# One read-out per chunk: the weights' products of all eight tiles in one PSUM bank

## The chip, the cores and the metric

The kernel runs on one core of a Trainium2 chip. The metric is the device time of one execution in microseconds; lower is better. Engines are named as in the profile: PE is the matrix engine (PEld its weight loads), DVE the vector engine, ACT the scalar engine, POOL the GpSimd engine, SP the engine whose queue issues most DMAs.

## The reference

Three stages follow one another, all in float32. Only the first is touched by the change:

```python
# r, k, v, w, a, b: [4, 8, 768, 40]  (batch, heads, time, dim)
for t in range(S):
    y[:, :, t] = np.einsum('bhd,bhde->bhe', rt, state)
    Sa = np.einsum('bhde,bhe->bhd', state, at)
    state_decay = state * wt[:, :, None, :] - np.einsum('bhd,bhe->bhde', Sa, bt)
    state = state_decay + np.einsum('bhd,bhe->bhde', vt, kt)
```

The second stage is a gated feed-forward block: `h = relu(x @ w_in)`, a convolution over three time steps, a sigmoid gate, `(h * gate) @ w_out`. The third is a causal attention with four experts of which each token uses two.

## The kernel before, in words

**Tiling.** The recurrence is computed in chunks of 32 time steps. `NT` = 12 blocks of 64 steps hold `NC` = 2 chunks each, so there are 24 chunks, k = 0 to 23. The 32 pairs of batch and head lie as 8 tiles (`NP`), each with two heads times two sides on the partitions.

**Streams.** The recurrence is written as generators, each of which yields the time at which its next piece is due (one block of 64 steps is 1.0): `prep(n)` makes the decay products and the triangular inverse of a block, mostly on DVE; `chain(k)` carries the state from chunk to chunk, mostly on PE and ACT; `post(k)` reads the outputs of a chunk out of the state; `ff` is the feed-forward stage, which starts while the recurrence still runs. `Kernel.merge` always takes the stream with the earliest due time and emits its next piece; `ff` is put in whenever the PE work counted so far (the first arguments of `mm` and `tr`) calls for it. So the order of the yields sets the order in which instructions are emitted; the framework's scheduler then orders them for each engine by its own estimate of when each is ready, and puts in the semaphores. On the chip each engine runs its instructions in that order. PSUM is one tensor of 8 banks of 512 float32 columns; `self.ps[j]` are pairs of banks.

**The read-out, `post(k)`**, due from k/2 + 0.5 on over half a block. It copies keys and state into `LB` by DMA, turns `U` with four transposes into `vp` and copies them to `VT` on ACT (L438). Then, for tiles 0 to 3 and again for tiles 4 to 7 (`p0` = 0 and 4):

- the weights' products (`ra` with `VT`, 8 matmul calls of 64x64) go into half a PSUM bank (256 columns), `ap`;
- two DVE multiplications (L448, one for each 64 partitions) bring them under the causal mask into `RB`.

After that the loads of `ra` and `VT` for the next chunk are issued, and again for `p0` = 0 and 4:

- the sums (`LB` with `RB`, 16 matmul calls) go into a half bank, `yp`;
- one DVE multiplication (L463) by the decay `P` writes them to `xe`.

Then the next `RB` is loaded, and after each second chunk `xe` goes to DRAM (L470), from where the feed-forward stage picks it up as `xd` (L537). Each matmul call in float32 appears as two MATMUL records. For chunks k >= 3 (`BK`) both products and sums of tiles 0 to 3 use the lower half of the bank `po` (the second bank of `ps[3]`), those of tiles 4 to 7 its upper half. For the first three chunks tiles 0 to 3 use `po` (products below, sums above) and tiles 4 to 7 a bank of `ps[1]`, which the feed-forward stage does not need yet. The memsets in `setup_a` clear the rows of these half banks that no sum writes and that the scaling reads.

Of the kernel before, what the change touches and what calls it, by code (L numbers as in the profile page):

```python
# [13 lines left out]
ALU = mybir.AluOpType  # L14
# [7 lines left out]
NP, NC = 8, 2  # L22

LEAST = float(np.array(0x38100000, np.int32).view(np.float32))
POST, FF, W0, W1, HB, WB, WT, REST, LW, LS, LT, LV, LR, LAG, BURST, Y0, Y1, EN, Y2, XA, GM, SC, UD, WF, WK, WS, WX, WD, WR, WV, WA, WY, GN, BK, FZ, FN, KQ, GU, LO = 0.5, 1.4, 0.2, 1, 4, 1, 12000, 1, 3.5, 1.0, 0.6, 0, -1.48, 1, 0.8, -0.4, 1.0, 3, 0, 30, 1, 0, 0, 20, 25, 34, 42, 59, 25, 54, -13, -29, 0, 3, 0, 3, 1, 0, 0
R = (slice(0, 40), slice(64, 104))
Z = (slice(0, 64), slice(64, 128))
E = slice(0, 104)
# [21 lines left out]
class Kernel:  # L50
# [7 lines left out]
    def setup_a(self, ctx):  # L58
        tc, nc = self.tc, self.nc
        cp = self.cp = ctx.enter_context(tc.tile_pool(name="acst", bufs=1))  # L60
        self.wk = ctx.enter_context(tc.tile_pool(name="awk", bufs=2))
        self.w = cp.tile([128, 32, 32], F32, name="w")
        self.kb = cp.tile([128, 16, 2, 2, 32], F32, name="kb")

        self.a = [cp.tile([128, 2, 2, 16, 32], F32, name=f"a{j}") for j in range(2)]
        self.SV = cp.tile([128, 2, 2, NP, 40], F32, name="SV")
        self.ra = cp.tile([128, NP, 2, 2, 32], F32, name="ra")

        self.LB = [cp.tile([128, 2, NP, 2, 40], F32, name=f"LB{j}") for j in range(2)]
        self.RB = cp.tile([128, 2, NP, 2, 32], F32, name="RB")  # L70
        self.P = [cp.tile([128, 32, 32], F32, name=f"P{j}") for j in range(3)]

        self.U = [cp.tile([128, NP // 2, 104], F32, name=f"U{j}") for j in range(2)]
        self.VZ = cp.tile([128, NP, 2, 2, 40], F32, name="VZ")
        self.VT = cp.tile([128, NP, 2, 64], F32, name="VT")
        self.sT = [cp.tile([128, NP, 104], F32, name=f"sT{j}") for j in range(2)]
        self.S = [cp.tile([128, NP, 2, 40], F32, name=f"S{j}") for j in range(2)]
        self.g21 = cp.tile([128, 8, 2, 16], F32, name="g21")
        self.d1 = cp.tile([128, 8, 32], F32, name="d1")
        self.M1 = cp.tile([128, 8, 2, 16], F32, name="M1")  # L80
        self.po = self.ps[3][:, 1].rearrange("p (a b) -> p a b", a=2)
        nc.vector.memset(self.w[32:64], 1.0)
        nc.gpsimd.memset(self.kb[32:64], 0.0)
        nc.gpsimd.memset(self.a[0][32:64], 0.0)
        nc.vector.memset(self.P[0][:, :, 0:1], 1.0)
        nc.vector.memset(self.po[:, 1], 0.0)
        nc.vector.memset(self.ps[1][:, 1, 256:], 0.0)
        cst = cp.tile([128, 164], F32, name="cst")
        self.ident, self.mask = cst[:, :128], cst[:, 128:160]
        self.m0, self.m1, self.m2 = cst[:, 160:161], cst[:, 161:162], cst[:, 162:163]  # L90
        self.cst = cst
        self.t = {}
        self.work = self.nn = 0
# [322 lines left out]
    def post(self, k):  # L416
        nc, wk, t = self.nc, self.wk, self.t[k // NC]
        n, c = divmod(k, NC)
        P, VT = t["P"], self.VT
        ra, LB, RB, u0 = self.ra, self.LB[k % 2], self.RB, NP * c  # L420
        for be in range(2):
            h = slice(64 * be, 64 * be + 64)
            nc.sync.dma_start(LB[h, be].rearrange("p u a d -> p (u a d)"), t["KB"][h, u0:u0 + NP].rearrange("p u a d -> p (u a d)"))
            if k:
                nc.sync.dma_start(LB[R[1 - be], be].rearrange("p u a d -> p (u a d)"),
                                  self.S[k % 2][R[be]].rearrange("p u a d -> p (u a d)"))
        if c == 0:
            t["xe"] = wk.tile([128, NP, 2, TOK], F32, name="xe", bufs=1)
        def po(p0, j):

            if k < BK:
                return (self.ps[1][:, 1].rearrange("p (a b) -> p a b", a=2) if p0 else self.po)[:, j]
            return self.po[:, p0 // 4]

        vp = (self.ps[1] if k < BK else self.ps[3])[:, 0].rearrange("p (u x) -> p u x", u=4)
        for p in range(4):
            self.tr(WV, vp[E, p], self.U[k % 2][:, p], self.ident)
        nc.scalar.activation(VT[E].rearrange("p u b x -> p (u b) x")[:, :, 32:], vp[E].rearrange("p u (b t) -> p (u b) t", t=32), AF.Copy)  # L438
        yield 0.16
        for p0 in range(0, NP, 4):  # L440
            ap = po(p0, 0).rearrange("p (u a t) -> p u a t", u=4, a=2)
            for p in range(4):
                for be in range(2):
                    self.mm(WA, ap[64 * be:64 * be + 64, p], VT[E, p0 + p, be], ra[E, p0 + p, be], start=True, stop=True)
            for be in range(2):
                s = slice(64 * be, 64 * be + 64)
                y = RB[s, be, p0:p0 + 4].rearrange("p u a t -> p (u a) t")
                nc.vector.tensor_tensor(y, ap[s].rearrange("p u a t -> p (u a) t"), self.mask[s, None].to_broadcast([64, 8, 32]), op=ALU.mult)  # L448
            yield 0.3 + 0.04 * p0
        if k + 1 < NT * NC:  # L450
            self.load_ra(k + 1)
            self.load_vt(k + 1)
        for p0 in range(0, NP, 4):
            yp = po(p0, 1).rearrange("p (m b t) -> p m b t", m=4, b=2)
            for p in range(4):
                for be in range(2):
                    r = slice(0, 104 + 24 * be)
                    for al in range(2):
                        self.mm(WY, yp[R[al], p, be], LB[r, be, p0 + p, al], RB[r, be, p0 + p, al], start=True, stop=True)
                if p % 2 == 1:  # L460
                    yield 0.55 + 0.05 * (p0 + p)
            pp = P.rearrange("p (c m b) t -> p c m b t", c=NC, b=2)[E, c, p0:p0 + 4]
            nc.vector.tensor_tensor(t["xe"][E, p0:p0 + 4, :, 32 * c:32 * c + 32], yp[E], pp, op=ALU.mult)  # L463
            yield 0.72 + 0.05 * p0
        if k + 1 < NT * NC:
            self.load_rb(k + 1)
        if c:
            xs = self.dp.tile([4, 2, 40, B, TOK], F32, name="xs", bufs=3)
            for al in range(2):
                nc.sync.dma_start(xs[:, al].rearrange("q e b t -> e b q t"),  # L470
                                    t["xe"][R[al]].rearrange("p (b h) c t -> p b (h c) t", b=B))
            t["xs"] = xs
        yield 1.0
# [557 lines left out]
```

## Time and profile before

| what | value |
|---|---|
| median of 3 runs | 901.09 us (898.76 to 907.43) |
| the profiled execution | 902.53 us, of which the span from the first to the last instruction is 900.8 us |
| busy: PE, PEld, DVE, ACT, POOL (whole span) | 756.9, 659.8, 699.4, 571.3, 365.6 us |
| mean granted PE clock | 0.929 of full speed |
| masking instructions L448 | 96, first at 73.3 us, last at 582.7 us |
| scaling instructions L463 | 48, first at 79.6 us, last at 586.2 us |

The read-out of the chunks runs from about 72 to 587 us; behind it the last pieces of the feed-forward stage and the attention follow, up to 900.8 us. The busy times are averages over stages with different limits: only what the first 587 us show bears on the change directly.

### The profile page before, as it was taken

How to read it: one execution, taken by the hardware profiler on the slowest of the kernel's cores; microseconds unless marked ns; L12 is line 12 of the kernel's file. 1: busy time of each engine (PE TensorE's matmuls, PEld its weight loads, DVE VectorE, ACT ScalarE, POOL GpSimd, SP SyncE). 2: the span in 40 equal slices, each digit the busy share in tenths (PEclk: the TensorE clock that was granted, in tenths of full speed). 3: DMA queues.
4: the chain of work that ended last, by engine and by line, in shares of the span. 5: the costliest groups of instructions: out<-in, count | busy, mean ns of one | idle time of the engine just before them, and what ended most of it. 6: DMA issues, size and time to landing. Idle time of an engine off the chain costs nothing.

```text
span 900.8 us, 31560 instructions
## 1 busy us (share of the span) xinstructions
PE 756.9 (84%) x13112; PEld 659.8 (73%) x13112; DVE 699.4 (78%) x1614; ACT 571.3 (63%) x1353; POOL 365.6 (41%) x419
## 2 busy tenths in 40 slices
PE   1257667988889988898988889959889989999988
PEld 1156556777778877787877779858778878888876
DVE  6888698798798989899898794656567776786664
ACT  1156556676676748584857577657767666776665
POOL 6163443434333324344333235564434353344353
PEclk9999568998898889998998899979999999999999
DMA  5434574545454556553646355250011100110001
GB/s 128 105 121 115 139 170 106 132 101 136 104 132 113 122 130 146 120 128 77 146 108 152 68 121 118 48 143 28 10 45 37 45 16 31 37 38 16 17 15 37
DMA packets 143488, 81.17 MB, mean 90 GB/s; under 512 B 113858, under 2 KB 127042, under 8 KB 142386
## 3 DMA queue, kind: packets, MB, share of 16 engines
q1 hardware_dynamic: 138450, 74.34, 33.8%
q0 software_dynamic: 4896, 4.83, 2.4%
q8 instruction: 103, 1.69, 0.8%
q14 instruction: 39, 0.32, 0.1%
HBM read 51.63 MB, written 11.80 MB: 70 GB/s over the span
## 4 chain that ended last, share of the span: by engine, by line
PE 38%; DVE 29%; ACT 10%; DMA 9%; issue 6%; POOL 4%; SPq 3%; POOLq 0%; ACTq 0%; DVEq 0%
PE ps L163 8%; PE ps L720 4%; DVE cv L604 4%; PE ps L823 4%; PE ps L569 4%; PE ps L806 4%; PE ps L592 3%; PE ps L167 2%; PE ps L770 2%; DVE RB L448 2%; PE ps L711 2%; DVE Q L200 2%; PE ps L838 2%; PE ps L771 2%; DVE a L211 2%
## 5 line engine op out<-in xcount | busy, mean ns | idle before, releaser
L792 POOL TENSOR_TENSOR A<-A,rs 128x128 f32<-128x128 f32 (+5 forms) x96 | 87.7, 936 | 106.3 <-DVE rs L790 61.3
L607 POOL TENSOR_TENSOR cv<-cv,h 128x512 f32<-128x512 f32 (+1 forms) x48 | 59.1, 1230 | 150.0 <-ACT cv L606 129.0
L604 DVE SCALAR_TENSOR_TENSOR cv<-h,cw,cv 128x256 f32<-128x256 f32 (+1 forms) x192 | 97.1, 546 | 25.0 <-ACT cv L602 21.9
L569 PE MATMUL ps<-xh,win 128*128 128x256 f32 x384 | 94.3, 302 | 5.8 <-ACT xh L545 4.2
L569 PE MATMUL ps<-xl,win 128*128 128x256 f32 x384 | 95.1, 300 | 0.5 <-POOL xl L546 0.4
L592 PE MATMUL ps<-wout,gh 128*128 128x320 f32 x384 | 90.5, 331 | 5.8 <-ACT gh L486 5.5
L777 ACT ACTIVATE A<-ps,nm 128x128 f32<-128x128 f32 (+5 forms) x96 | 60.8, 634 | 35.8 <-DVE nm L775 26.8
L487 POOL TENSOR_TENSOR gl<-cv,gh 128x512 fp32r<-128x512 f32 x48 | 62.6, 1305 | 44.6 <-ACT gh L486 44.0
L569 PEld LDWEIGHTS ps<-xh,win 128*128 128x128 f32 x384 | 71.3, 204 | 7.9 <-ACT xh L545 4.7
L592 PEld LDWEIGHTS ps<-wout,gh 128*128 128x128 f32 x384 | 66.2, 201 | 8.3 <-ACT gh L486 6.8
L569 PEld LDWEIGHTS ps<-xl,win 128*128 128x128 f32 x384 | 70.9, 202 | 1.8 <-POOL xl L546 0.8
L775 DVE TENSOR_REDUCE nm<-ps 128x1 f32<-128x128 f32 (+5 forms) x96 | 58.6, 619 | 16.9 <-PE ps L773 10.8
L163 PE MATMUL ps<-kb,a 40*32 40x64 f32 x1536 | 39.2, 254 | 32.7 <-DVE kb L207 29.4
L592 PE MATMUL ps<-wout,gl 128*128 128x320 f32 x192 | 59.4, 332 | 0.9 <-POOL gl L487 0.9
L163 PE MATMUL ps<-RB,LB 104*40 104x32 f32 (+1 forms) x1536 | 50.6, 213 | 11.1 <-DVE RB L448 6.9
L163 PEld LDWEIGHTS ps<-kb,a 40*32 40x32 f32 x1536 | 30.9, 129 | 37.6 <-issue 19.2
L163 PEld LDWEIGHTS ps<-RB,LB 104*40 104x40 f32 (+1 forms) x1536 | 42.2, 127 | 20.5 <-DVE RB L448 9.0
L720 PE MATMUL ps<-x,wqk 128*128 128x384 f32 x256 | 54.5, 353 | 2.8 <-DVE lg L714 2.4
L606 ACT ACTIVATE cv<-cv 128x512 f32<-128x512 f32 (+1 forms) x48 | 30.3, 630 | 39.8 <-DVE cv L604 39.5
L806 PE MATMUL ps<-cid,A 128*128 128x128 f32 x336 | 53.0, 277 | 2.2 <-POOL A L792 1.5
L770 PE MATMUL ps<-k,q 128*128 128x256 f32 (+3 forms) x144 | 49.5, 352 | 3.6 <-ACT A L777 3.3
L163 PE MATMUL ps<-ra,VT 104*64 104x64 f32 x768 | 43.8, 255 | 8.4 <-DVE RB L448 6.8
(178 smaller groups left out, 2177.7 us busy)
## 6 DMA issues: line engine op xcount, KB each, us to landing
kb<-in_kb_e_dram SPq DMA_DIRECT2D x24, 320.0 KB
LB<-KB SPq DMA_DIRECT2D x48, 160.0 KB
LB<-S SPq DMA_DIRECT2D x46, 100.0 KB
a<-in_a_e_dram SPq DMA_DIRECT2D x24, 160.0 KB
VT<-in_vt_dram SPq DMA_DIRECT2D x48, 80.0 KB
RB<-in_rb_dram SPq DMA_DIRECT2D x48, 80.0 KB
SV<-in_v_dram SPq DMA_DIRECT2D x48, 80.0 KB
VZ<-in_v_dram SPq DMA_DIRECT2D x96, 40.0 KB
```

The costliest lines, as they stand in the source:

```text
L163: self.nc.tensor.matmul(*a, **k)
L487: (eng or self.nc.vector).tensor_tensor(lo, x, hi.bitcast(F32), op=ALU.subtract)
L569: nc.tensor.matmul(hp[:, dd], wt[:, 128 * d:128 * d + 128], x, start=k == 0, stop=k == 7)
L592: nc.tensor.matmul(self.ps[1][:, tb, :DM], x, wt, start=d == 0 and k == 0, stop=d == 7 and k == 2)
L604: nc.vector.scalar_tensor_tensor(y, h[:, dd, :, k:k + nt], self.cw[:, k, d:d + 1], y, op0=ALU.mult, op1=ALU.add)
L607: (nc.gpsimd if GM and st % GM == 0 and st >= GN else nc.vector).tensor_tensor(cv[:, :, :, :nt], cv[:, :, :, :nt], h[:, :, :, 1:1 + nt], o ...
L720: nc.tensor.matmul(pp, self.wqk[:, wk, hl, 128 * m:128 * m + 128], x[:, xk], start=j == 0, stop=j == 7)
L770: nc.tensor.matmul(sp[:, c0:c1], q[:, ce, 128 * j:128 * j + 128], k[:, ce, c0:c1], start=True, stop=False)
L775: nc.vector.tensor_reduce(nm, sp[:, :nk], axis=AX.X, op=ALU.max, negate=True)
L777: nc.scalar.activation(A[:, :nk], sp[:, :nk], AF.Exp, bias=nm, accum_out=sums[:, e:e + 1])
L792: nc.gpsimd.tensor_tensor(A[:, :nk], A[:, :nk], rs[:, e:e + 1].to_broadcast([128, nk]), op=ALU.mult)
L806: nc.tensor.transpose(tp[:, m, e], As[e][:, 128 * (2 * g + m):128 * (2 * g + m) + 128], self.cid)
```

## The change

The two halves of the read-out become one. All eight tiles' products fill one whole bank (the second of `ps[3]`, 512 columns), two masking instructions of 64x512 follow, then all eight tiles' sums fill a whole bank (for the first three chunks one of `ps[1]`, later the same bank of `ps[3]`), and one scaling instruction of 104x512 follows. The matmuls, the DMAs and their counts stay as they were. The yields become fewer: within the products there is one after tile 3 (0.3), the masking is emitted behind the last product; the sums yield after tiles 3 and 7 (0.70 and 0.90), where they yielded after each second tile (0.60, 0.70, 0.80, 0.90). The two memsets of half a bank become one of a bank.

```diff
--- before.py
+++ after.py
@@ -78,13 +78,11 @@
         self.g21 = cp.tile([128, 8, 2, 16], F32, name="g21")
         self.d1 = cp.tile([128, 8, 32], F32, name="d1")
         self.M1 = cp.tile([128, 8, 2, 16], F32, name="M1")
-        self.po = self.ps[3][:, 1].rearrange("p (a b) -> p a b", a=2)
         nc.vector.memset(self.w[32:64], 1.0)
         nc.gpsimd.memset(self.kb[32:64], 0.0)
         nc.gpsimd.memset(self.a[0][32:64], 0.0)
         nc.vector.memset(self.P[0][:, :, 0:1], 1.0)
-        nc.vector.memset(self.po[:, 1], 0.0)
-        nc.vector.memset(self.ps[1][:, 1, 256:], 0.0)
+        nc.vector.memset(self.ps[1][:, 1], 0.0)
         cst = cp.tile([128, 164], F32, name="cst")
         self.ident, self.mask = cst[:, :128], cst[:, 128:160]
         self.m0, self.m1, self.m2 = cst[:, 160:161], cst[:, 161:162], cst[:, 162:163]
@@ -426,42 +424,36 @@
                                   self.S[k % 2][R[be]].rearrange("p u a d -> p (u a d)"))
         if c == 0:
             t["xe"] = wk.tile([128, NP, 2, TOK], F32, name="xe", bufs=1)
-        def po(p0, j):
-
-            if k < BK:
-                return (self.ps[1][:, 1].rearrange("p (a b) -> p a b", a=2) if p0 else self.po)[:, j]
-            return self.po[:, p0 // 4]
-
         vp = (self.ps[1] if k < BK else self.ps[3])[:, 0].rearrange("p (u x) -> p u x", u=4)
         for p in range(4):
             self.tr(WV, vp[E, p], self.U[k % 2][:, p], self.ident)
         nc.scalar.activation(VT[E].rearrange("p u b x -> p (u b) x")[:, :, 32:], vp[E].rearrange("p u (b t) -> p (u b) t", t=32), AF.Copy)
         yield 0.16
-        for p0 in range(0, NP, 4):
-            ap = po(p0, 0).rearrange("p (u a t) -> p u a t", u=4, a=2)
-            for p in range(4):
-                for be in range(2):
-                    self.mm(WA, ap[64 * be:64 * be + 64, p], VT[E, p0 + p, be], ra[E, p0 + p, be], start=True, stop=True)
+        ap = self.ps[3][:, 1].rearrange("p (u a t) -> p u a t", u=NP, a=2)
+        for p in range(NP):
             for be in range(2):
-                s = slice(64 * be, 64 * be + 64)
-                y = RB[s, be, p0:p0 + 4].rearrange("p u a t -> p (u a) t")
-                nc.vector.tensor_tensor(y, ap[s].rearrange("p u a t -> p (u a) t"), self.mask[s, None].to_broadcast([64, 8, 32]), op=ALU.mult)
-            yield 0.3 + 0.04 * p0
+                self.mm(WA, ap[64 * be:64 * be + 64, p], VT[E, p, be], ra[E, p, be], start=True, stop=True)
+            if p == 3:
+                yield 0.3
+        for be in range(2):
+            s = slice(64 * be, 64 * be + 64)
+            y = RB[s, be].rearrange("p u a t -> p (u a) t")
+            nc.vector.tensor_tensor(y, ap[s].rearrange("p u a t -> p (u a) t"), self.mask[s, None].to_broadcast([64, 2 * NP, 32]), op=ALU.mult)
+        yield 0.46
         if k + 1 < NT * NC:
             self.load_ra(k + 1)
             self.load_vt(k + 1)
-        for p0 in range(0, NP, 4):
-            yp = po(p0, 1).rearrange("p (m b t) -> p m b t", m=4, b=2)
-            for p in range(4):
-                for be in range(2):
-                    r = slice(0, 104 + 24 * be)
-                    for al in range(2):
-                        self.mm(WY, yp[R[al], p, be], LB[r, be, p0 + p, al], RB[r, be, p0 + p, al], start=True, stop=True)
-                if p % 2 == 1:
-                    yield 0.55 + 0.05 * (p0 + p)
-            pp = P.rearrange("p (c m b) t -> p c m b t", c=NC, b=2)[E, c, p0:p0 + 4]
-            nc.vector.tensor_tensor(t["xe"][E, p0:p0 + 4, :, 32 * c:32 * c + 32], yp[E], pp, op=ALU.mult)
-            yield 0.72 + 0.05 * p0
+        yp = (self.ps[1] if k < BK else self.ps[3])[:, 1].rearrange("p (m b t) -> p m b t", m=NP, b=2)
+        for p in range(NP):
+            for be in range(2):
+                r = slice(0, 104 + 24 * be)
+                for al in range(2):
+                    self.mm(WY, yp[R[al], p, be], LB[r, be, p, al], RB[r, be, p, al], start=True, stop=True)
+            if p % 4 == 3:
+                yield 0.55 + 0.05 * p
+        pp = P.rearrange("p (c m b) t -> p c m b t", c=NC, b=2)[E, c]
+        nc.vector.tensor_tensor(t["xe"][E, :, :, 32 * c:32 * c + 32], yp[E], pp, op=ALU.mult)
+        yield 0.92
         if k + 1 < NT * NC:
             self.load_rb(k + 1)
         if c:
```

## Rows read from the trace of the kernel before

**Rows 1.** Stretches: us, busy time (and instructions) per engine, granted clock, DMA

```profile
core 0: us, PE busy (x) PEld busy (x) DVE busy (x) ACT busy (x) POOL busy (x), PEclk, DMA share, GB/s
60.00:120.00 60.00, 42.65 (x880) 34.93 (x882) 48.52 (x108) 36.25 (x78) 24.65 (x30) 0.72 0.50 130
200.00:300.00 100.00, 90.27 (x2153) 79.29 (x2155) 86.66 (x185) 67.53 (x148) 35.28 (x39) 0.90 0.51 119
400.00:500.00 100.00, 85.12 (x2026) 75.94 (x2011) 91.43 (x185) 67.75 (x150) 38.15 (x41) 0.91 0.54 125
800.00:901.00 101.00, 93.67 (x817) 78.32 (x815) 62.43 (x183) 61.53 (x164) 42.36 (x46) 0.99 0.08 26
```

**Rows 2.** Chain that ended last: start, us, what; first and last of L448, L463

```profile
104.64 0.38 DVE RB L448
...
116.51 0.33 DVE xe L463
...
582.71 0.44 DVE RB L448
...
586.19 0.43 DVE xe L463
```

**Rows 3.** One chunk's read-out in time: start, us, engine, line, operation [idle before]

```profile
338.63 0.33 PE L163 MATMUL ps<-ra,VT 104*64 104x64 f32 x2
...
339.70 0.85 DVE L448 TENSOR_TENSOR RB<-ps,cst 64x256 f32<-64x256 f32 x2
...
341.67 0.69 PE L163 MATMUL ps<-ra,VT 104*64 104x64 f32 x16
...
343.95 0.86 DVE L448 TENSOR_TENSOR RB<-ps,cst 64x256 f32<-64x256 f32 x2
...
345.63 0.50 PE L163 MATMUL ps<-RB,LB 104*40 104x32 f32 x16
...
350.47 0.43 DVE L463 TENSOR_TENSOR xe<-ps,P 104x256 f32<-104x256 f32 x1
...
350.95 0.80 PE L163 MATMUL ps<-RB,LB 104*40 104x32 f32 x32 [1.21 <-DVE xe L463]
```

**Rows 4.** By line: ns min/median/max of masking, scaling, a 512-column multiplication

```profile
L448 DVE TENSOR_TENSOR RB<-ps,cst x96: 371/427/431, 73.3 to 582.7; 64x256 f32<-64x256 f32 x96
L463 DVE TENSOR_TENSOR xe<-ps,P x48: 376/415/433, 79.6 to 586.2; 104x256 f32<-104x256 f32 x48
L291 DVE TENSOR_TENSOR t<-TT,G x12: 681/692/846, 39.6 to 531.4; 128x512 f32<-128x512 f32 x12
```

**Rows 5.** DVE in order of time: start to start of neighbours that overlap

```profile
115.03 0.67 DVE L292 TENSOR_REDUCE N<-t 128x64 f32<-128x512 f32 x1
115.63 0.48 DVE L505 SCALAR_TENSOR_TENSOR wx<-wy,wx 128x320 int32<-128x320 int32 x1
...
116.43 0.41 DVE L463 TENSOR_TENSOR xe<-ps,P 104x256 f32<-104x256 f32 x1
116.76 1.00 DVE L288 TENSOR_TENSOR t<-N,TT 128x512 f32<-128x512 f32 x1
```

**Rows 6.** Tile ra: idle before its products (us, times; PE plus PEld)

```profile
  DVE RB L448: 14.5, 11
```

**Rows 7.** Tile LB: idle before its sums (us, times); who waited for them

```profile
  DVE RB L448: 15.9, 19
  DVE xe L463: 8.5, 6
...
  DVE xe L463: 9.6, 4
```

## The prediction

> **What bounds the kernel now.** I read the stretches first. Between 200 and 500 us DVE is the busiest engine (86.7 us of 100 in the first stretch shown, 91.4 in the last), PE close behind it (90.3 and 85.1) [rows 1]. Neither is full, so this is no stage with one limit: PE waits for DVE and DVE for PE by turns. After 800 us PE is busy for 93.7 of 101 us and the read-out is long over; that stage can only be moved, not shortened. What is won or lost is therefore won before 587 us, and the question is which of the read-out's own times lie on the path there.
>
> The chain that ended last answers it. Added up over 60 to 590 us, of the 96 masking instructions 50 lie on it with 19.3 us, of the 48 scalings 16 with 5.1 us; the first and the last of each are in [rows 2]. So about half of the masks and a third of the scalings are paid for in the end; the rest is hidden behind PE, ACT or DMA.
>
> Then I read one chunk in order of time [rows 3]. Products of tiles 0 to 3 end at 338.96, their two masks run at 339.70; products of the other tiles start at 341.67, masks at 343.95; first sums at 345.63, scaling at 350.47, and the second sums start at 350.95, after 1.21 us in which PE stood still for the scaling. These second sums write the upper half of the bank while the scaling reads the lower half: nothing in the data orders the two, so the wait goes by the whole bank. The same holds for the second products behind the first masks. A chunk has thus four turns from PE to DVE and back, one behind the other, and not two that overlap. That is the row on which my sign rests.
>
> **The change part by part.** *Fewer DVE instructions.* A mask of 256 columns takes 427 ns, a scaling 415 ns, and a DVE multiplication of 512 columns takes 692 ns [rows 4]; I take 692 ns for both new forms. Two masks become one: 2 x 427 - 692 = 162 ns less, 48 times in 24 chunks, 7.8 us. Two scalings become one: 2 x 415 - 692 = 138 ns, 24 times, 3.3 us. Together 11.1 us of DVE work. That is the upper bound, since neighbours on DVE can overlap: a scaling of 0.41 us was followed after 0.33 us by the next start (116.43 to 116.76), and a 512-column instruction of 0.67 us after 0.60 us (115.03 to 115.63) [rows 5]. By starts an instruction removed gives 2 x 0.33 - 0.60 = 0.06 us, 72 times 4.3 us; that is the lower bound. The pair of masks in the chunk shown takes 0.85 and 0.86 us, that is twice the full duration [rows 3], so for the masks I take the 162 ns.
>
> What the Trainium skill says on this, in "Perfetto Trace Analysis", section "Optimizing Scalar/DVE Operations", is that a DVE instruction pays about 125 ns on PSUM beside its elements. By that the 72 removed ones would give an estimate of 9.0 us, between the two bounds above.
>
> *What of it is on the path.* Masks: 7.8 us x 50/96 = 4.1 us. Scalings: 3.3 us x 16/48 = 1.1 us. Sum 5.2 us. If everything removed counted, it would be 11.1 us; if only the lower bound at the chain's shares, 48 x 0.06 x 0.52 + 24 x 0.06 x 0.33 = 2.0 us.
>
> *The waits.* Idle time before the products that ended with a mask is 14.5 us [rows 6], and before the sums that ended with a scaling 8.5 us [rows 7]. These figures count PE and its weight loads each, so I halve them (an estimate): 7.2 and 4.2 us, 11.4 us of PE's standstill. Both kinds of wait go, since the second half of products and of sums no longer has DVE work in front of it. What is late next is the first sum. It now waits for both wide masks, 2 x 0.692 = 1.38 us instead of the last pair's 0.85 us, so 0.53 us more. The sums waited for a mask 19 times, again with PE and PEld both counted, so in about 10 chunks [rows 7]: 10 x 0.53 = 5.3 us come back at least, and if every chunk had no slack 24 x 0.53 = 12.7 us. The emitted order leaves as much between masks and first sum as before (0.3 to 0.46 of half a block), so I stay near the lower figure, 8 us. The net is 11.4 - 8 = 3.4 us, between 6.1 us gained and 1.3 us lost. Part of it is the same time as the masks on the chain, which are there because PE waited for them; I count 1.5 us of it.
>
> *What queues behind.* Behind the first sum on PE stand the feed-forward matmuls and the next chain's products; behind the masks on DVE stand the inverse's small steps and the convolution, whose results ACT and PE want. Those are held up by a lump of 1.38 us in place of two of 0.85 us; in total they have 2 x 0.85 - 1.38 = 0.33 us less in front of them. SP's queue has the same DMAs in the same order; the loads of `ra` and `VT` may start sooner, since the products end without a wait in the middle. The scaling waited four times for the sums, 9.6 us [rows 7]; it is now emitted 0.20 of half a block behind the first half of the sums, and its only wait is for the last sum. I count this as nothing: behind it stands `xe`'s way to DRAM, which the last scaling delays by 0.692 - 0.415 = 0.28 us and the removed turn brings forward by as much or more. The memset at the start is one instead of two and lies before the first chunk. The granted clock was 0.72 of full speed at 60 to 120 us and 0.90 and 0.91 in the middle stretches, where it is a mix of the two levels of 1.2 and 2.4 GHz [rows 1]; a steadier PE could raise it, but I have no row that prices this, and leave it out of the sum.
>
> *The sum.* 5.2 + 1.5 = 6.7 us less than the profiled execution's 902.53 us is 895.8 us; that execution lies 1.4 us above the median of the runs shown, which is within their scatter of 8.7 us. I predict 896 us.
>
> **The rivals.** *The whole saving counts.* DVE is the busiest engine, and if it sets the pace throughout, all 11.1 us go, and the 3.4 us of waits with them: 902.5 - 14.5 = 888 us; with the larger net of waits, 6.1 us, 885.3 us. For it: 91.4 us of 100 in [rows 1]. Against it: only half of the masks are on the chain [rows 2].
>
> *Nothing arrives.* The saved time on DVE goes into waits for ACT or for DMAs that end at the same moment as before: 2.0 us at the lower bound, 900.5 us. For it: PE, DVE, ACT and DMA take turns on the chain, so that the next one in line can hold the end.
>
> *The lump costs more than the turns did.* The place is the first sum of each chunk: PE is then held until two wide masks are done, with nothing of the second half to run meanwhile. Price: 12.7 us if all chunks have no slack; and with it the convolution and the inverse's small steps, held by the longer lump, come up to 0.53 us late in each chunk. If none of the old waits had been on the path and the saving on the chain stays, 902.5 - 5.2 + 12.7 = 910.0 us; without that saving 915.2 us. It decides from the point at which more than 6.7/0.53 = 13 chunks meet the lump unhidden without an old wait removed in exchange. For it: half of the masks lie on the chain already, and the scheduler's estimate, not the chip, put other work between. Against it: the turns that go cost 11.4 us. The Trainium skill has a rule that speaks for this rival, in "Perfetto Trace Analysis", section "Optimizing Scalar/DVE Operations": where these engines aren't saturated but cause bubbles on others, breaking instructions up may let work end sooner. By that rule the wider masks are the wrong way round, and the trace agrees in so far as neither engine is full.
>
> **How the numbers follow.** My forecast, 896 us with a range of its own of 891 to 900, has 0.40. The whole saving has 0.23, nothing arriving 0.14, the lump 0.23: the order for each engine is worked out anew by the scheduler's estimate, and its waits can fall worse as well as better, which is why I keep the last one this high. The range must reach into both outer cases: 885 us from the larger waits below, 912 us between the lump's two prices above. About a change of 1% is what a measurement of this kernel can tell from none; that is 892.1 and 910.1 us. Faster by more: the whole saving and the lower edge of the forecast, 0.28. Slower by more: most of the lump, 0.22. Within it 0.50.
>
> **What would show it.** In the profile after, L448's successor should come 48 times at about 0.69 us, L463's 24 times at about 0.69 us, with DVE's busy time about 11 us lower. The idle time before the products that ended with a mask should be gone, and that before the sums that ended with a scaling too; that of the sums behind a mask should be longer each. The last scaling should begin some 5 to 7 us before 586.2 us. I am wrong if the masks take much more than 0.7 us, if the idle before the sums grows past 11 us of PE, or if the read-out ends later while DVE is idler: then the order of the queues has decided and not the work.

## The result and the profile after

The changed kernel takes 896.14 us (median of 18 runs, 887.33 to 902.01), the kernel before 903.1 us in as many runs beside it (898.26 to 910.15). The ratio is 0.9911 with a 95% interval of 0.9882 to 0.994: 0.0089 x 903.1 = 8.0 us less, at least 5.4 and at most 10.7 us. The ratio leaves out runs in the chip's slower state, two of the 18 of the changed kernel, so it isn't that of the two medians, which differ by 7.0 us. The profiled execution took 899.17 us, of which the span is 897.4 us; it lies 3 us above the median, so that its own difference to the profiled execution of before is only 3.4 us.

First the two kinds of instruction that the change makes wider, by tile (duration in ns, minimum, median, maximum, then first and last start):

```profile
L441 DVE TENSOR_TENSOR RB<-ps,cst x48: 646/688/696, 79.2 to 571.4; 64x512 f32<-64x512 f32 x48
L455 DVE TENSOR_TENSOR xe<-ps,P x24: 647/688/700, 89.3 to 574.7; 104x512 f32<-104x512 f32 x24
```

The idle time before the products, by tile `ra` (us, times, PE and PEld each counted), and then before the sums, by tile `LB`, with what ended it:

```profile
  ACT VT L430: 7.8, 7
```

```profile
  DVE RB L441: 7.9, 8
  issue: 6.3, 7
  DMA RB<-in_rb_dram: 5.6, 3
```

Against [rows 4] there are half as many of each, at 688 ns where two took 854 and 830 ns. Against [rows 6] the products wait for no mask any more; the wait is not there at all, and what ends their idle time is ACT's copy of `VT`. Against [rows 7] the sums no longer wait for a scaling, and their idle behind a mask, 15.9 us in 19 counts, is 7.9 us in 8.

The same chunk as in [rows 3], in order of time, shows two turns instead of four:

```profile
337.40 0.57 PE L161 MATMUL ps<-ra,VT 104*64 104x64 f32 x12
...
340.80 1.36 DVE L441 TENSOR_TENSOR RB<-ps,cst 64x512 f32<-64x512 f32 x2
...
342.22 0.50 PE L161 MATMUL ps<-RB,LB 104*40 104x32 f32 x14 [0.16 <-DMA ra<-in_ra_dram]
...
345.07 1.18 PE L161 MATMUL ps<-RB,LB 128*40 128x32 f32 x50
...
348.50 0.69 DVE L455 TENSOR_TENSOR xe<-ps,P 104x512 f32<-104x512 f32 x1
```

The lump of two masks is 1.36 us long. From the last product (its group ends at 337.97) to the lump's end at 342.16 more than 4 us pass, but PE has other work meanwhile: its idle before the first sum is 0.16 us. And it does not stand still for the scaling. It does stand still between the sums, 1.85 us before 344.56 us, for another reason: a copy of `KB` on ACT.

On the chain that ended last the wide masks are much rarer than in [rows 2]: 14 of 48 with 9.0 us, where it was 50 of 96 with 19.3 us; of the scalings 7 of 24 with 4.5 us. The last of each (start, us, what):

```profile
571.38 0.69 DVE RB L441
...
574.73 0.70 DVE xe L455
```

So the read-out ends at 574.7 us where it ended at 586.2: 11.5 us earlier. The span is only 3.4 us shorter. The stretches, to be read against those of [rows 1], show more (us, busy time and instructions of each engine, granted clock, DMA share, GB/s):

```profile
200.00:300.00 100.00, 84.81 (x2038) 75.07 (x2037) 87.21 (x164) 64.82 (x141) 39.54 (x41) 0.86 0.55 126
...
400.00:500.00 100.00, 83.54 (x2103) 75.78 (x2102) 83.41 (x171) 65.66 (x147) 34.88 (x38) 0.88 0.54 126
```

DVE is less busy in the second stretch shown (83.4 instead of 91.4 us), about as busy in the first (87.2 instead of 86.7), and PE is busy for less time in both. The granted clock is lower in both: 0.86 and 0.88, where it was 0.90 and 0.91. More feed-forward work is left over when the read-out ends. Counted in matmuls of L569 (L561 after) from the last scaling on (us, PE busy and instructions, clock, DMA), first the kernel before, then the changed one:

```profile
586.20:700.00 113.80, 15.82 (x112) 0.94 0.19 52
```

```profile
574.70:700.00 125.30, 22.59 (x160) 0.96 0.19 50
```

The read-out has run ahead of the feed-forward stage: 160 of its 768 input matmuls are still to come instead of 112. The last of them begins at 641.1 us, where it was 637.0 (last start in the rows of the kernel before and of the changed one):

```profile
L569 PE MATMUL ps<-xh,win x384: 274/283/583, 137.0 to 637.0; 128*128 128x256 f32 x192
```

```profile
L561 PE MATMUL ps<-xh,win x384: 274/283/582, 134.4 to 641.1; 128*128 128x256 f32 x192
```

From there to the end of the span it takes 256.3 us instead of 263.8. The attention had begun earlier beside it: its projection L712 (L720 before) begins at 607.3 us instead of 618.8. So in this pair of executions 4.1 us are lost up to the last input matmul and 7.5 us won behind it, which makes the 3.4 us.

### The profile page after: what moved, and what is told of

It reads as the page before. It is cut to its first block, busy times and chain, and to the rows that moved or that the text cites. A ratio compares the mean times of both kernels' runs of the same rounds, so it can differ in the third digit from the quotient of the medians.

```text
span 897.4 us, 31509 instructions
## 1 busy us (share of the span) xinstructions
PE 748.3 (83%) x13112; PEld 657.7 (73%) x13112; DVE 693.9 (77%) x1541; ACT 574.4 (64%) x1355; POOL 377.6 (42%) x419
## 4 chain that ended last, share of the span: by engine, by line
PE 42%; DVE 24%; ACT 11%; DMA 10%; issue 7%; POOL 4%; SPq 1%; ACTq 0%; DVEq 0%; POOLq 0%
PE ps L161 8%; PE ps L561 5%; PE ps L584 5%; PE ps L815 4%; DVE cv L596 4%; PE ps L712 4%; PE ps L798 4%; PE ps L165 3%; PE ps L703 2%; PE ps L762 2%; PE ps L830 2%; DMA kb<-in_kb_e_dram 2%; DVE kb L205 2%; PE ps L763 2%; DVE Q L198 2%
## 5 line engine op out<-in xcount | busy, mean ns | idle before, releaser
L599 POOL TENSOR_TENSOR cv<-cv,h 128x512 f32<-128x512 f32 (+1 forms) x48 | 61.4, 1280 | 133.2 <-ACT cv L598 123.6
L561 PE MATMUL ps<-xl,win 128*128 128x256 f32 x384 | 97.1, 304 | 4.5 <-POOL xl L539 3.6
L561 PE MATMUL ps<-xh,win 128*128 128x256 f32 x384 | 96.5, 309 | 4.9 <-ACT xh L537 4.3
L769 ACT ACTIVATE A<-ps,nm 128x128 f32<-128x128 f32 (+5 forms) x96 | 60.7, 633 | 37.0 <-DVE nm L767 28.9
L561 PEld LDWEIGHTS ps<-xh,win 128*128 128x128 f32 x384 | 73.2, 210 | 7.0 <-ACT xh L537 4.6
L561 PEld LDWEIGHTS ps<-xl,win 128*128 128x128 f32 x384 | 73.1, 208 | 6.0 <-POOL xl L539 4.1
L161 PE MATMUL ps<-kb,a 40*32 40x64 f32 x1536 | 34.3, 239 | 34.7 <-DVE kb L205 31.1
L165 PE MATMUL ps<-cst,kb 104*128 104x104 f32 x192 | 33.3, 307 | 29.4 <-ACT KB L265 16.4
L161 PE MATMUL ps<-RB,LB 104*40 104x32 f32 (+1 forms) x1536 | 47.9, 215 | 11.1 <-DMA RB<-in_rb_dram 5.0
L161 PEld LDWEIGHTS ps<-kb,a 40*32 40x32 f32 x1536 | 28.1, 120 | 39.0 <-issue 19.1
L712 PE MATMUL ps<-x,wqk 128*128 128x384 f32 x256 | 53.2, 347 | 0.3 <-ACT yt L622 0.3
L598 ACT ACTIVATE cv<-cv 128x512 f32<-128x512 f32 (+1 forms) x48 | 30.3, 630 | 30.7 <-DVE cv L596 30.4
```

The source lines that it names most:

```text
L161: self.nc.tensor.matmul(*a, **k)
L165: self.nc.tensor.transpose(*a)
L561: nc.tensor.matmul(hp[:, dd], wt[:, 128 * d:128 * d + 128], x, start=k == 0, stop=k == 7)
L599: (nc.gpsimd if GM and st % GM == 0 and st >= GN else nc.vector).tensor_tensor(cv[:, :, :, :nt], cv[:, :, :, :nt], h[:, :, :, 1:1 + nt], o ...
L712: nc.tensor.matmul(pp, self.wqk[:, wk, hl, 128 * m:128 * m + 128], x[:, xk], start=j == 0, stop=j == 7)
L769: nc.scalar.activation(A[:, :nk], sp[:, :nk], AF.Exp, bias=nm, accum_out=sums[:, e:e + 1])
```

## The experiments

**The same work in another order.** The scheduler lays out the order on each engine by its own estimate, from the order of emission. An edit that changes nothing but the order of emission lays out every queue anew: the traces of the changed kernel and of the first of the following hold the same 13112 matmul records in another order. It is the changed kernel with the finer yields of before:

```diff
-            if p % 4 == 3:
+            if p % 2 == 1:
                 yield 0.55 + 0.05 * p
```

> The changed kernel with the same instructions, but the sums yield after each second tile as in the kernel before. Work, turns and instruction counts are those of the changed kernel; only the order in which the pieces are emitted differs. Theory of the prediction: 896 us within 2. Rival 'order decides': differs from the changed kernel by 4 us or more either way. It also gives the scatter against which the other experiments are to be read.

Measured: 913.7 us, 1.0088 of the kernel before (1.0054 to 1.0122), so 1.0088 / 0.9911 = 1.018 of the changed kernel. Same instructions of the program, same two turns, 1.8% slower. Its row for the scaling, by tile `xe`, and its feed-forward matmuls left over, as counted above:

```profile
L455 DVE TENSOR_TENSOR xe<-ps,P x24: 649/683/693, 91.4 to 551.4; 104x512 f32<-104x512 f32 x24
```

```profile
551.40:700.00 148.60, 35.49 (x250) 0.91 0.18 49
```

Its read-out ends another 23 us earlier than that of the changed kernel, and 250 matmuls are left over instead of 160. The rival that the order decides has its first point.

The opposite step is the kernel before with the coarse yields of the changed one:

```diff
-                if p % 2 == 1:
+                if p % 4 == 3:
                     yield 0.55 + 0.05 * (p0 + p)
```

> The kernel before with the sums' yields of the changed kernel (after each fourth tile): the same instructions as before, only emitted in another order. Theory of the prediction: 903 us within 2. Rival 'the yields, that is the order, made the gain': near 896 us. Rival 'any order is a new draw': differs from the kernel before by 4 us or more either way.

Measured: 906.95 us, 1.0054 (1.0023 to 1.0086). The yields alone don't make the gain; they cost half a per cent here. With the coarse yields in both kernels the change gains 1.4% (0.9911 / 1.0054 = 0.986); with the fine ones in both it costs 0.9%.

A second pair moves the due time of the whole read-out by 0.02 of a block, in both kernels:

```diff
-POST, FF, W0, ... = 0.5, 1.4, 0.2, ...
+POST, FF, W0, ... = 0.52, 1.4, 0.2, ...
```

> The kernel before with the whole read-out due 0.02 of a block later (POST 0.52 instead of 0.50): the same instructions, and the order on every engine laid out anew. A second new draw of the kernel before. If the structure sets the time: 903 us within 2. If any new order is a draw and the kernel before was a good one: 903 to 920 us.

> The changed kernel with the same step (POST 0.52). If the structure sets the time: 896 us within 2, and 7 us under the kernel before with the same step. If any new order is a draw and the changed kernel was a good one: 896 to 920 us, without relation to the run beside it.

Measured: the kernel before with the step 903.98 us, 1.004 (1.0008 to 1.0073); the changed kernel with it 912.33 us, 1.0106 (1.0058 to 1.0154). With this due time the change costs 0.7% instead of gaining 0.9%. The changed kernel's read-out again ends early, at 561.8 us, with 208 matmuls left over; that of the kernel before at 585.7 with 114. The row of the changed kernel:

```profile
561.80:700.00 138.20, 30.39 (x208) 0.93 0.19 49
```

So three orders of the old read-out lie within 0.6% of each other, and three of the new one between 0.9911 and 1.0106; two more of the new one, below under `WT`, have 1.0171 and 1.0111.

**The order kept.** To price DVE time by itself, the finished program was edited behind the scheduler: each mask instruction but the first few is replaced by one over 18 of each 32 columns, with the same semaphores. The order on PE, ACT, POOL and SP is then that of the kernel edited, and on DVE too; the 13112 matmul records of the first trace below come in exactly the order of the kernel before.

```diff
     with tile.TileContext(nc, schedule_with_timeline_sim=True) as tc:
         Kernel(tc, ins, {"out": out}).run()
+    narrow_masks(nc, 18, 8)
```

```python
ap[-1] = [1, width]
return M.PhysicalAccessPattern(ap=ap, offset=p.offset, dtype=p.dtype, memref=p.memref, memsetref=p.memsetref)
...
b.instructions[j] = M.InstTensorTensor(
    op=i.op, ...
    sync_info=i.sync_info, ...)
```

> The kernel before with its order kept: the scheduler sees the same instructions, and only in the finished program the masks (all but the first eight) are cut from 256 to 144 columns, so that 14 of each 32 columns are left unmasked and stale. Order, waits, turns and counts on every engine are those of the kernel before; DVE has 88 x 112 columns less, at the 1.04 ns per column of the rows of before (692 - 427 ns over 256 columns) 10.3 us less, about what the change takes away. Theory of the prediction (half of the masks' time is on the path): 5 us less than before, 897 to 899 us. Rival 'DVE sets the pace': 10 us less, 892 us. Rival 'what the read-out saves is hidden, the order decides': 902 to 904 us, as before.

Measured: 897.99 us, 0.9957 (0.9922 to 0.9992), which is 3.9 us less, between 0.7 and 7.0 (the two medians, 897.99 and 901.32, differ by 3.3). The narrow masks take 311 ns instead of 427; below them its scaling and the matmuls left over:

```profile
L448 DVE TENSOR_TENSOR RB<-ps,cst x96: 253/311/428, 72.7 to 576.9; 64x144 f32<-64x144 f32 x88, 64x256 f32<-64x256 f32 x8
```

```profile
L463 DVE TENSOR_TENSOR xe<-ps,P x48: 375/414/427, 79.1 to 580.3; 104x256 f32<-104x256 f32 x48
```

```profile
580.30:700.00 119.70, 17.00 (x112) 0.93 0.19 51
```

88 x 0.116 = 10.2 us less on DVE gave 3.9 us, a share of 0.38, with an interval of 0.07 to 0.69, which holds the chain's share of 0.52 and leaves out "all" and, narrowly, "nothing". In the profiled execution the read-out ends 5.9 us earlier, the same 112 matmuls are left, and the span is 5.6 us shorter: with the order kept, what the read-out gains reaches the end in this pair.

The same edit in the changed kernel, `narrow_masks(nc, 18, 4)`:

> The changed kernel with its order kept, and in the finished program the masks (all but the first four) cut from 512 to 288 columns; 14 of each 32 columns are left unmasked and stale. DVE has 44 x 224 columns less, again about 10.3 us. The chain of the changed kernel holds 14 of its 48 masks with 9.0 of 32.8 us. Theory that the chain's share prices DVE time (0.27): 3 us less than the changed kernel, 893 us. Rival 'hidden': 896 us. Rival 'DVE sets the pace': 886 us.

Measured: 894.01 us, 0.989 (0.9854 to 0.9926) of the kernel before; the changed kernel has 0.9911 (0.9882 to 0.994). The difference of 0.0021, some 1.9 us, is smaller than the half-width of either interval. It fits the 3 us of the chain's share and does not exclude that nothing is left to gain; 10 us are excluded.

**The parts of the change.** Only the products and masks joined, the sums in halves again:

```diff
+        for p0 in range(0, NP, 4):
+            for p in range(p0, p0 + 4):
             ...
+            nc.vector.tensor_tensor(t["xe"][E, p0:p0 + 4, :, 32 * c:32 * c + 32], yp[E, p0:p0 + 4], pp, op=ALU.mult)
+            yield 0.72 + 0.05 * p0
```

> Only the products and masks are joined (one bank, two wide masks); the sums keep two halves, two scalings and the turn between them. Theory of the prediction: the masks' 4.1 us and the turn behind the first masks come, the scalings' 1.1 us and the turn behind the first scaling don't: about 898 us. Rival 'only turns': 899 us, with idle before the sums that ended with a scaling back near 8 us (PE and PEld together). Rival 'order decides': 890 to 906 us without relation to e3.

Only the sums and the scaling joined, the products in halves with their masks behind each:

```diff
+        for p0 in range(0, NP, 4):
+            for p in range(p0, p0 + 4):
             ...
+            for be in range(2):
+                s = slice(64 * be, 64 * be + 64)
+                y = RB[s, be, p0:p0 + 4].rearrange("p u a t -> p (u a) t")
                 ...
+            yield 0.3 + 0.04 * p0
```

> Only the sums and the scaling are joined; the products keep two halves with two narrow masks behind each. Theory of the prediction: about 900 us (1.1 us of the scalings and the turn behind the first scaling). The two parts e2 and e3 should add up to the whole change. Rival 'only turns': 900 us, idle before the products that ended with a mask back near 14 us. Rival 'order decides': 890 to 906 us, and the parts don't add up.

Measured: 925.98 us, 1.0246 (1.0206 to 1.0287), for the first, and 907.55 us, 1.0035 (1.0009 to 1.0061), for the second. Neither part is faster, and they don't add up to the whole. In the first the idle before the sums behind a scaling is 19.0 us in 21 counts, where [rows 7] has 8.5: this wait can indeed be far dearer than in the kernel before.

```profile
  DVE xe L456: 19.0, 21
```

That accounts for some 5 us (half of the 10.5 more, since PE and PEld are both counted) of 0.0246 x 905.33 = 22 us; the rest isn't explained.

The turns joined, but the DVE work in small instructions:

```diff
+            for p0 in range(0, NP, 4):
+                y = RB[s, be, p0:p0 + 4].rearrange("p u a t -> p (u a) t")
+                nc.vector.tensor_tensor(y, ap[s, p0:p0 + 4]...
```

> The changed kernel with its two turns per chunk kept, but the DVE work cut small again: four masking instructions of 64x256 and two scalings of 104x256 behind the whole bank. Theory of the prediction (half of the removed DVE time lies on the path, 5.2 us; the removed turns give 1.5 us): about 901 us. Rival 'only the removed turns count': as the changed kernel, 896 us within 2. Rival 'only the number of DVE instructions counts': as the kernel before, 903 us. Rival 'the order for each engine decides' (any edit makes the scheduler lay out all queues anew): anywhere from 890 to 906 us, with the masks' share on the chain saying nothing about it.

Measured: 931.36 us, 1.0302 (1.0253 to 1.035). No theory gave this much. The products wait for no mask here either, so the turns are gone, and the 11 us of DVE time that came back can't make the 35 us by which it is slower than the changed kernel. It is a new order as well, with 221 matmuls left over at 574.2 us. What its two differences are worth can't be told from it.

**Two that missed their aim.** Additional DVE work in the changed kernel, this line twice behind the masks and once behind the scaling:

```diff
+        nc.vector.tensor_reduce(self.dum, self.mask[:, None].to_broadcast([128, 4, 32]), axis=AX.X, op=ALU.add)
```

> The changed kernel with three further DVE instructions per chunk that nobody waits for (a sum over 4 x 32 columns of the mask, some 0.25 to 0.3 us each, two behind the masks and one behind the scaling): about 20 us more DVE work, twice what the change took away, with the turns left as they are. Theory of the prediction (half of DVE's time is on the path): 906 us, 10 us more than the changed kernel. Rival 'only turns': 896 to 898 us. Rival 'DVE sets the pace': 914 to 916 us.

Measured: 927.37 us, 1.0282 (1.0253 to 1.031). But nothing held these instructions in place, and the scheduler put them all early (one of three lines, which are alike):

```profile
L443 DVE TENSOR_REDUCE dum<-cst x24: 250/279/289, 10.4 to 96.7; 128x4 f32<-128x128 f32 x24
```

They ran before 100 us instead of beside the masks. It says nothing on the price of DVE time in the read-out; it is one more order.

The feed-forward stage emitted earlier, by a smaller `WT`, 11500 and 11000 in place of 12000:

```diff
-POST, FF, W0, W1, HB, WB, WT, ... = 0.5, 1.4, 0.2, 1, 4, 1, 12000, ...
+POST, FF, W0, W1, HB, WB, WT, ... = 0.5, 1.4, 0.2, 1, 4, 1, 11500, ...
```

> The changed kernel with the feed-forward stage emitted a little earlier (WT 11500 instead of 12000). In the profile of the changed kernel the read-out ends 11.5 us earlier, but the whole only 3.4 us: at that point about 0.8 of a block of the feed-forward stage more is still to do than before. If this backlog took back the rest, less of it at the end of the read-out makes the kernel faster: 890 to 893 us. If the backlog is hidden behind the attention: 896 us within 2. If the earlier feed-forward work only delays the recurrence: 897 to 901 us.

> The same with WT 11000, that is twice the shift. If the backlog takes back part of the gain: 887 to 892 us. If it is hidden: 896 us within 2. If it only delays the recurrence: 899 to 906 us. A jump without relation to the first step speaks for 'the order decides'.

Measured: 917.32 us, 1.0171 (1.0128 to 1.0213), and 912.27 us, 1.0111 (1.007 to 1.0151). With 11500 the emission was earlier and yet 192 matmuls were left over instead of 160; with 11000 there were 120, but the read-out ended at 592.3 us. The setting doesn't steer the backlog alone, so the experiment neither shows nor refutes that less of it would help. Both are two further orders of the changed kernel's instructions, and both are slower than the kernel before.

## Why the prediction was right, and where it was not

**The number.** 896 us was forecast and 896.14 measured; 6.7 us less was the sum, 8.0 us (5.4 to 10.7) the result. That is closer than its steps deserve: steps that were off by several us cancelled, and that was luck, as follows.

**Fewer DVE instructions: right in size.** The groups of DVE by line and shape, 60 to 590 us (count, busy us, mean ns, idle before), of the kernel before and then of the changed one:

```profile
L448 DVE TENSOR_TENSOR RB<-ps,cst 64x256 f32<-64x256 f32 x96 | 40.2, 419 | 5.2 <-PE ps L163 3.9
...
L463 DVE TENSOR_TENSOR xe<-ps,P 104x256 f32<-104x256 f32 x48 | 19.8, 413 | 10.9 <-PE ps L163 9.6 <-DMA xs<-xe 1.1
```

```profile
L441 DVE TENSOR_TENSOR RB<-ps,cst 64x512 f32<-64x512 f32 x48 | 32.8, 684 | 4.6 <-PE ps L161 4.1
...
L455 DVE TENSOR_TENSOR xe<-ps,P 104x512 f32<-104x512 f32 x24 | 16.5, 685 | 9.4 <-PE ps L161 9.2
```

The masks sum to 32.8 us instead of 40.2, the scalings to 16.5 instead of 19.8: 10.7 us less, where 11.1 was worked out from the 512-column row in [rows 4]. The lower bound from the overlapping starts in [rows 5] did not apply. DVE's busy time over the whole span, however, fell only from 699.4 to 693.9 us, by 5.5 where about 11 was forecast: the other DVE instructions, the same in number but for one memset, took 4.6 us more in sum. Why is not shown.

**What of it is on the path: borne out, roughly.** The chain's share of 0.52 for the masks made 4.1 us of 7.8. With the order kept, 10.2 us less DVE time gave 3.9 us, a share of 0.38 with a wide interval. That interval leaves out the rival in which the whole saving counts. The rival in which nothing arrives was priced at 2.0 of 11.1 us, a share of 0.18, and that lies inside it; only zero is left out, narrowly. What speaks against that rival is the whole change, whose 8.0 us are at least 5.4. The other half of these 8.0 us cannot be divided between the turns that went and the new order. One reading was wrong without bearing on the sum: between 200 and 300 us PE (90.3 us) and not DVE (86.7) is the busier engine.

**The waits: gone as said, but the lump was mis-sized.** The idle of the products behind a mask (14.5 us) and that of the sums behind a scaling (8.5 us) are gone, and they are gone in every order of the joined read-out, while the two other orders of the old one have 10.3 and 6.8 us of the former, 6.2 and 6.9 us of the latter. The first sums' wait for the wide masks, which I had grow by 5.3 to 12.7 us, fell instead: 7.9 us in 8 counts instead of 15.9 in 19, per count 0.99 us instead of 0.84 (PE and PEld are both in these figures). Each wait is a little longer, but far fewer meet it. In the chunk above, other PE work stands between products and sums. In the four other orders of the joined read-out this wait is 5.3 to 9.3 us in 9 to 13 counts; but the kernel before with its due time shifted has 8.8 us in 10 counts too, so the fall may come from the order and not from the joining. With 8 us saved there instead of lost, halved as in the prediction 4 us, the net of the waits would have been 15.4 instead of 3.4 us. But other waits took their place: all causes of idle before the sums together went only from about 27 to 25 us, with 5.6 us for the load of `RB` and 4.6 us for a convolution step on DVE new among them. The scaling's own wait for the sums, which the prediction counted as nothing, stayed: 9.2 us where it was 9.6. The rival of the lump is not what happened in this kernel. The rule of the Trainium skill that stood beside it, in "Perfetto Trace Analysis", section "Optimizing Scalar/DVE Operations", that breaking instructions up may help where they cause bubbles on other engines, finds no support here: PE and PEld idle 7.9 us behind the wider masks, not more than the 15.9 us before. As the order changed with the width, it is no clean test of the rule.

**The last scaling: forecast 5 to 7 us earlier, measured 11.5.** The read-out gained nearly double, and the sum came out since part of it was given back later. The step that failed is the sentence that what is won before 587 us reaches the end, as the stage behind it "can only be moved". It was not merely moved: from the last scaling to the end of the span it took 314.6 us before and 322.7 after. The feed-forward stage runs beside the read-out, and what it has not done when the read-out ends still has to be done. From the last scaling to the last input matmul it took 50.8 us with 112 left over before, 66.4 with 160 after, 103.9 with 250 and 92.7 with 208 in the first two other orders: 0.42 to 0.45 us for each. The remaining orders of both kernels and the runs with narrow masks have 0.39 to 0.46. The end of the program goes with the feed-forward stage rather than with the read-out: in all fourteen traces the span ends 253 to 268 us after the last input matmul begins, but 307 to 361 us after the last scaling. That these go together is read from the traces; that the backlog causes the loss was not shown, since the experiment meant to reduce it did not do so.

**What the prediction left too small: the order.** I had given the order a sentence, as a reason for the chance of the lump. It is a term of its own, and larger than my sum. The changed kernel's instructions in four other orders take 1.0088, 1.0106, 1.0111 and 1.0171 of the kernel before, the old ones in two other orders 1.0054 and 1.004. So the gain of 0.9% belongs to the joined read-out in the order that it happened to get, which is the best of five. With the order of the kernel before kept, a DVE saving of this size is worth about 4 us; that the joined read-out is faster whatever the order was not found, and in the pairs with the shifted due time and with the fine yields it is slower.

One thing does change with the order although no line of the kernel does. ACT_TABLE_LOAD, 1.28 us each, stands in the traces on ACT wherever it goes from the gate's sigmoid (L598) to the attention's exponentials (L729, L769) and back, that is, while feed-forward and attention run side by side. The loads at the gate, in the changed kernel and in its first other order:

```profile
L598 ACT ACT_TABLE_LOAD  x4: 1283/1283/1283, 149.5 to 643.4; - x4
```

```profile
L598 ACT ACT_TABLE_LOAD  x9: 1283/1283/1283, 144.8 to 661.5; - x9
```

In all, the kernel before has 7 of these loads and the changed kernel 9; six of the seven runs at 1.0088 and above have 15 to 19, every other run at most 9. In the order with the shifted due time 10 of them, 12.6 us, lie on the chain that ended last, in the changed kernel 3. That makes them a candidate for a part of what a poor order costs, not shown as its cause: the run with `WT` 11000 has 9 and is at 1.0111, and no run varied them alone.

The granted clock, which the prediction left out of its sum, did not rise: 0.923 over the whole span instead of 0.929. What that cost is not worked out.

Why most orders of the joined read-out leave more of the feed-forward stage over, I can only argue: without the inner turns the scheduler's estimate lets the read-out, and with it the recurrence, run further ahead.

None of the runs is shown to beat the changed kernel; the narrow masks that come out at 894.01 us leave part of the work out.

## What to carry to other kernels

Where two steps take turns on one PSUM bank, joining the halves removed both the turns and a fixed 0.15 us for each DVE instruction that went; the chain's share of the instruction (here 0.52) as a price for the latter is not contradicted by the one run that kept the order (0.38, between 0.07 and 0.69). But where a scheduler lays out the queues by its own estimate, take the change's instructions in two or three other orders before believing a gain of a per cent, and price a single cost by editing the finished program, where the order stays. And ask of a stage that ends sooner what ran beside it and is left over: of the 11.5 us, 3.4 reached the end in the profiled pair, and 8.0 us are the gain by the ratio of all runs.

## What the runs showed of the hardware beyond that

A multiplication of 512 columns on 64 partitions out of PSUM takes 688 ns, as long as one of 512 columns on 128 partitions out of SBUF does (692 ns, L291 in [rows 4]). The 112 columns cut off a mask took 427 - 311 = 116 ns with them, 1.04 ns each, so that a mask's fixed part is 427 - 256 x 1.04 = 161 ns: it is per instruction and nearly the same in the wide, the old and the narrow form (688 - 512 x 1.04 = 156 ns, 311 - 144 x 1.04 = 161 ns).
